# The first 17 microseconds of a fused layernorm, state-space and MLP kernel: reciprocal root on GpSimd, tile 0 scaled by ScalarE, and first matmuls on one x tile

## The chip, the cores and the metric

The kernel runs on one core of a Trainium2 chip. The metric is the device time of one execution in microseconds (us). Besides its time, each timed execution has a span, from its first to its last instruction, which is 1.2 to 1.5 us shorter than the time.

PE is the matrix engine (TensorE), PEld its weight loads, DVE is VectorE, ACT is ScalarE, POOL is GpSimd.

## The reference

The input x is 2048 tokens of 1024 values. It is normalised, and the result goes through a diagonal state-space layer (a recurrence over the tokens) and through a two-layer MLP. Their sum, with x, is the output.

```python
def _layernorm(x, axis=-1, eps=1e-5):
    m = jnp.mean(x, axis=axis, keepdims=True)
    v = jnp.var(x, axis=axis, keepdims=True)
    return (x - m) / jnp.sqrt(v + eps)

# ... _A_ref: complex diagonal recurrence, 1024 states
# ... _B_ref: h = x @ w1 + b1 (3584 wide); act = h * tanh(softplus(h)); act @ w2
    xn = _layernorm(x, axis=-1)
    return x + _A_ref(xn, ...) + _B_ref(xn, ...)
```

## The kernel before

The tokens are worked on in four blocks of 512, each of four x tiles of 128 tokens. Nearly all of the time is a stream of matmuls. Before the stream can start, PE needs normalised and transposed x and the first weights. This stage, the head, is what the change rewrites.

In the head, each x tile passes these steps: its load; `bn_stats` of both halves and `bn_aggr` on VectorE (mean and variance); a root of the variance and a reciprocal; the scaling `(x - m) * y`; eight 128x128 transposes on PE into PSUM; and a copy to SBUF (`xnT`). The weights come in 512 KB ring tiles. Ring tiles 0 and 1 hold the upper and lower half of the contraction (k from 0 to 3, and from 4 to 7) for the weight tiles f = 0 to 3; ring tiles 2 and 3 do so for f = 4 to 7.

Filler matmuls (`keep_busy`) on zeros keep PE occupied while it waits; they are meant to have its clock full when the stream starts.

```python
    def first_sqrt(q):
        aop(lambda e: e.activation(rc(q, 1), mv[:, q, 1:2], AF.Sqrt, bias=kon[:, 2:3]), ...)      # ScalarE

    def first_apply(q, pieces=1):
        y = rc(q, 1)
        vop(lambda e: e.reciprocal(y, y), ...)                                                    # VectorE
        for h in range(pieces):
            ...
            vop(lambda e, d=d: e.tensor_scalar(xn[:, q, d], xx[:, 0, q, d], mv[:, q, 0:1], y,
                                               op0=ALU.subtract, op1=ALU.mult), ...)              # VectorE
    ...
    keep_busy(40)
    for q in range(2):
        first_sums_v(q, 0); first_sums_v(q, 1); first_var_v(q); first_sqrt(q)
    keep_busy(20, [b_mv[0]])          # waits for tile 0's variance
    # transpose of the small parameters on PE
    keep_busy(10, [b_mv[1]])
    first_apply(0)
    first_transpose(0)
    first_apply(1, 2)
    first_transpose(1)
    keep_busy(8)
    # copies of tiles 0 and 1; then statistics, root, scaling of tiles 2 and 3, in this order:
    #   sums 2, var 2, root 2, half of sums 3, scale 2, other half of sums 3, var 3, root 3, scale 3
    for f in range(4):
        first_half(f, 0, 0, NK // 2)                  # tokens of tiles 0 and 1: 256 columns, k 0..3
    for f in range(4):
        first_half(f, 0, NK // 2, NK)                 # k 4..7
        if f == 2:
            first_transpose(2); first_copy(2, AC)
    first_half(4, 0); first_transpose(3); first_copy(3, VE); first_half(5, 0)
    # then the other 256 columns of f = 0..5, and from f = 6 on matmuls of 512 columns
```

"Tokens are columns" here: a matmul of 256 columns covers two x tiles. The layernorm of later blocks (`ln_rsqrt`, a reciprocal root made of 15 VectorE instructions, and `ln_root`, ScalarE's root for block 1) is far from the head.

## Time and profile before

| | before |
|---|---|
| first 3 executions | 621.52 us median (621.43 to 622.23) |
| 6 executions (3 more with the changed kernel) | 621.86 us median (621.43 to 623.07) |
| profiled execution | 621.25 us, span 619.8 us |
| first useful matmul in that profile | 8.55 us |
| stream reaches the second 256 columns of f = 0 | 14.79 us |

The last row is the record of the ninth matmul there, at 14.897 us, less the 0.109 us of a missing record. In this profile every fiftieth matmul or so has no record, and this leaves gaps of exactly two spacings.

These are the span, the busy times and the chain that ended last, from the page of the kernel before.

```profile
span 619.8 us, 7370 instructions
...
PE 613.6 (99%) x2925; PEld 288.3 (47%) x2981; DVE 463.1 (75%) x678; ACT 246.6 (40%) x158; POOL 50.4 (8%) x47
...
PE 95%; ACT 2%; DVE 2%; issue 1%; DVEq 0%
```

PE is busy 99% of the span and holds 95% of the chain. Nothing but PE counts, as long as PE is fed.

This is PE's timeline of the head in the same profile (start us, duration us, engine, line, operation, output and input, count).

```profile
5.02 1.28 PE L463 MATMUL ps<-filler 128*128 128x128 bf16 x20
...
7.02 1.24 PE L379 MATMUL ps<-ident,xn 128*128 128x128 bf16 x16
...
8.55 3.22 PE L509 MATMUL ps<-xnT,ring 128*128 128x256 bf16 x28
11.60 0.61 PE L379 MATMUL ps<-ident,xn 128*128 128x128 bf16 x8
...
13.41 0.61 PE L379 MATMUL ps<-ident,xn 128*128 128x128 bf16 x8
13.86 3.82 PE L509 MATMUL ps<-xnT,ring 128*128 128x256 bf16 x32
```

L463 is the fillers, L379 transposes, L509 the first useful matmuls. From 8.55 us on the entries touch each other: single matmuls start 0.109 us apart (256 columns), transposes 0.056 us apart. So only what lies before 8.55 us can be saved.

This is VectorE's timeline and then ScalarE's one line for the same tile 3, kernel before.

```profile
4.55 0.21 DVE L355 BATCH_NORM_AGGREGATE mv<-stats 128x2 f32<-128x12 f32 x1
...
6.14 0.21 DVE L355 BATCH_NORM_AGGREGATE mv<-stats 128x2 f32<-128x12 f32 x1
...
6.42 0.55 DVE L367 TENSOR_SCALAR xn<-xx,mv,rs 128x1024 bf16<-128x1024 bf16 x1
...
7.98 0.42 DVE L392 COPY xnT<-ps 128x512 bf16<-128x512 bf16 x1 [0.17 <-PE ps L379]
...
11.93 0.21 DVE L355 BATCH_NORM_AGGREGATE mv<-stats 128x2 f32<-128x12 f32 x1
12.50 0.16 DVE L363 RECIPROCAL rs<-rs 128x1 f32<-128x1 f32 x1 [0.36 <-ACT rs L358]
12.70 0.55 DVE L367 TENSOR_SCALAR xn<-xx,mv,rs 128x1024 bf16<-128x1024 bf16 x1
```

```profile
12.17 0.30 ACT L358 ACTIVATE rs<-mv,kon 128x1 f32<-128x1 f32 x1 [1.76 <-DVE mv L355]
```

L355 is the end of a tile's statistics. For tile 3 they end at 11.93 + 0.21 = 12.14 us, ScalarE's root and VectorE's reciprocal follow, and scaling (L367) starts at 12.70: 0.56 us. For tile 0 the scaling waits in VectorE's queue for tile 1's statistics and starts at 6.42 although tile 0's variance was done at 4.76.

### The profile page before, as it was taken

What the parts mean: (1) busy time and instruction counts of PE and PEld (TensorE: products, weight loads), DVE (VectorE), ACT (ScalarE), POOL (GpSimd) and SP (SyncE); (2) the same over time, 40 slices, a digit from 0 to 9 for tenths busy, and PEclk for the clock granted to TensorE, in tenths of its full rate; (3) what the DMA queues carried; (4) which work ended last, traced back from release to release, by engine and by line L of the source; (5) the groups of instructions that cost most, each with busy time, mean ns of one, the idle gap of its engine ahead of it and who ended that gap; (6) DMA issues with size and microseconds to landing.
All of it is one profiled execution on the core that took longest, in us unless ns stands there. A gap on an engine that the chain in (4) does not pass through costs nothing.

```text
span 619.8 us, 7370 instructions
## 1 busy us (share of the span) xinstructions
PE 613.6 (99%) x2925; PEld 288.3 (47%) x2981; DVE 463.1 (75%) x678; ACT 246.6 (40%) x158; POOL 50.4 (8%) x47
## 2 busy tenths in 40 slices
PE   9999999999999999999999999999999999999998
PEld 8544444444444444444444444444444444444444
DVE  6897999999467599998147659999624856999603
ACT  4779996440079940000009992000001999000000
POOL 1999000000100000000010000000000000000000
DMA  8999986840464401783064430276203541033001
GB/s 289 243 214 296 208 160 190 219 136 1 134 194 147 136 1 35 195 209 105 17 186 137 146 126 1 82 205 176 82 34 106 167 169 69 0 122 116 1 0 69
DMA packets 95948, 79.41 MB, mean 128 GB/s; under 512 B 48938, under 2 KB 78506, under 8 KB 95914
## 3 DMA queue, kind: packets, MB, share of 16 engines
q1 hardware_dynamic: 92416, 71.64, 42.3%
q0 software_dynamic: 960, 3.15, 2.2%
q10 hardware_dynamic: 2538, 4.14, 1.8%
q8 instruction: 24, 0.39, 0.3%
q14 instruction: 10, 0.08, 0.0%
HBM read 63.19 MB, written 4.19 MB: 109 GB/s over the span
## 4 chain that ended last, share of the span: by engine, by line
PE 95%; ACT 2%; DVE 2%; issue 1%; DVEq 0%
PE ps L733 49%; PE ps L654 26%; PE ps L675 18%; PE ps L463 1%; PE ps L509 1%; ACT act L635 1%; ACT act L634 1%; ACT act L633 1%; DVE hb L662 0%; DVE stats L350 0%; DVE act L640 0%; PE ps L747 0%; ACT L634 0%; ACT L525 0%; ACT xnT L390 0%
## 5 line engine op out<-in xcount | busy, mean ns | idle before, releaser
L733 PE MATMUL ps<-ring,act 128*128 128x512 bf16 x880 | 193.2, 379 | 0.8
L654 PE MATMUL ps<-xnT,ring 128*128 128x512 bf16 x832 | 182.7, 379 | 0.8
L633 ACT ACTIVATE act<-hb 128x3584 bf16<-128x3584 bf16 x16 | 50.9, 3183 | 224.0 <-DVE hb L662 223.7
L733 PEld LDWEIGHTS ps<-ring,act 128*128 128x128 bf16 x896 | 87.7, 98 | 105.7
L654 PEld LDWEIGHTS ps<-xnT,ring 128*128 128x128 bf16 x848 | 83.0, 98 | 99.9
L662 DVE TENSOR_SCALAR hb<-ps,par 128x512 bf16<-128x512 f32 x112 | 82.2, 747 | 54.6 <-PE ps L654 53.4
L675 PE MATMUL ps<-xnT,BT 128*128 128x512 bf16 x500 | 110.5, 379 | 0.6
L733 PE MATMUL ps<-CT,hT 128*128 128x512 bf16 x494 | 109.2, 379 | 0.6
L680 DVE TENSOR_TENSOR mt<-ps,tab 128x1024 bf16<-128x1024 f32 x64 | 75.4, 1220 | 17.2 <-PE ps L675 16.5
L675 PEld LDWEIGHTS ps<-xnT,BT 128*128 128x128 bf16 x512 | 50.1, 98 | 60.4
L733 PEld LDWEIGHTS ps<-CT,hT 128*128 128x128 bf16 x506 | 49.5, 98 | 59.7
L698 DVE TENSOR_TENSOR_SCAN hT<-cs,qi,hT 128x512 bf16<-128x512 f32 x48 | 58.9, 1269 | 0.0
L778 DVE TENSOR_TENSOR xx<-ps,xx 128x1024 bf16<-128x1024 f32 (+1 forms) x16 | 18.8, 1190 | 46.3 <-PE ps L733 46.2
L634 ACT ACTIVATE act<-act 128x3584 bf16<-128x3584 bf16 x16 | 51.0, 3190 | 0.2
L635 ACT ACTIVATE act<-act 128x3584 bf16<-128x3584 bf16 x16 | 51.0, 3190 | 0.2
L703 DVE TENSOR_TENSOR mt<-hT,tab 128x1024 bf16<-128x1024 bf16 x64 | 41.4, 688 | 1.1
L640 DVE TENSOR_TENSOR act<-act,hb 128x3584 bf16<-128x3584 bf16 x16 | 32.3, 2018 | 1.3 <-ACT act L635 1.3
L287 POOL DMA_DIRECT2D xx<-in_A_x_dram x12 | 6.7, 560 | 254.4 <-DVE xx L778 247.9
L609 ACT ACTIVATE ct<-CT,cs 128x512 f32<-128x512 bf16 x16 | 11.5, 721 | 26.0 <-DVE CT L611 25.9
L634 ACT ACT_TABLE_LOAD x16 | 20.5, 1283 | 0.3
L635 ACT ACT_TABLE_LOAD x16 | 20.5, 1283 | 0.3
L698 DVE TENSOR_TENSOR_SCAN hT<-cs,hT 128x512 bf16<-128x512 f32 x16 | 18.7, 1208 | 0.0
(81 smaller groups left out, 279.2 us busy)
## 6 DMA issues: line engine op xcount, KB each, us to landing
ring<-in_B_w_dram SPq DMA_DIRECT2D x112, 512.0 KB, 4.2
out_dram<-xx ACTq DMA_DIRECT2D x15, 256.0 KB, 2.1
xx<-in_A_x_dram POOLq DMA_DIRECT2D x12, 256.0 KB, 4.6
xx<-in_A_x_dram SPq DMA_DIRECT2D x4, 128.0 KB, 2.2
xx<-in_A_x_dram SPq DMA_DIRECT2D x2, 256.0 KB, 5.2
dsk<-in_A_Dskip_dram SPq DMA_DIRECT2D x1, 256.0 KB, 9.3
xnT<-xn SPq DMA_TRANSPOSE x12, 4.7
BT<-in_A_B_re_dram SPq DMA_TRANSPOSE x8, 6.3
```

Source lines behind the costliest of these rows:

```text
L633: aop(lambda e: e.activation(a, hs, AF.Exp), reads=[b_hb[g % 2]], writes=[b_act[g]])
L634: aop(lambda e: e.activation(a, a, AF.Ln, bias=1.0), reads=[b_act[g]], writes=[b_act[g]])
L635: aop(lambda e: e.activation(a, a, AF.Tanh), reads=[b_act[g]], writes=[b_act[g]])
L640: vop(lambda e: e.tensor_tensor(a, a, hs, op=ALU.mult), reads=[b_act[g], b_hb[g % 2]], writes=[b_act[g]])
L654: PE.mm(lambda e, k=k, w=w: e.matmul(ps[:, bank, :], lhsT=w, rhs=xnT[:, k, :], start=k == 0, stop=k == NK - 1), reads=[b_ring[s]] + b_xnT, ...
L662: vop(lambda e: e.tensor_scalar(hb[:, hs, :], ps[:, bank, :], b1(f), None, op0=ALU.add), reads=[b_ps[bank], b_par], writes=[b_hbf[hs]])
L675: PE.mm(lambda e, j=j, ci=ci, k=k, bank=bank: e.matmul(ps[:, bank + ci, :], lhsT=BT[:, ci, j, k, :], rhs=xnT[:, k, :], start=k == 0, stop= ...
L680: vop(lambda e, s=s, u=u, j=j: e.tensor_tensor(mt[:, s, :, :], u, tab[:, s, j, :].unsqueeze(1).to_broadcast([P, 2, TB]), op=ALU.mult), rea ...
L698: vop(lambda e, ci=ci, init=init: e.tensor_tensor_scan(out=hT[:, ci, j, :], data0=cj("r", j).to_broadcast([P, TB]), data1=hT[:, ci, j, :], ...
L703: vop(lambda e, s=s: e.tensor_tensor(mt[:, s, :, :], hT[:, :, j, :], tab[:, s, j, :].unsqueeze(1).to_broadcast([P, 2, TB]), op=ALU.mult), ...
L733: PE.mm(lambda e: e.matmul(ps[:, u, :], lhsT=lhsT, rhs=rhs, start=st_, stop=last), reads=reads, writes=[b_ps[u]], first=st_, last=last)
L778: vop(lambda e: e.tensor_tensor(xr, src, xr, op=ALU.add), reads=b_ps[bank:bank + n] + [b_x], writes=[b_x])
```

## The change

It means to start the stream earlier, with tile 0 alone. GpSimd computes the reciprocal root as a power of -0.5, so VectorE and ScalarE's tables are not needed for it. ScalarE scales tile 0 while VectorE is still at tile 1's statistics. The first weight tiles run on tile 0's 128 tokens while tile 1 is finished. Since tile 0 and tile 1 now accumulate at different times in one PSUM bank, four matmuls of zeros open the banks. x tile 1 is loaded in one piece instead of two, the loads of x tiles 2 and 3 come after the second ring tile, f = 6 joins the split (`NSPLIT`), fillers are fewer, and the later layernorms use GpSimd's power as well. The core of the diff:

```diff
-    for q in range(2):
-        for h in range(2):
-            SP.dma(... x tile q, half h ...)
+    for h in range(2):
+        SP.dma(... x tile 0, half h ...)
+    load_x(SP, 0, 1)
...
-        if i < 2:
-            load_x(SP, 0, 2 + i)
+        if i == 1:
+            load_x(SP, 0, 2)
+            load_x(SP, 0, 3)
...
-    def first_sqrt(q): ...                     # ScalarE root; reciprocal was in first_apply
+    def first_rstd(q, negated_mean=False):
+        pop(lambda e: e.tensor_scalar(rc(q, 0), mv[:, q, 1:2], EPS, None, op0=ALU.add), ...)
+        pop(lambda e: e.tensor_tensor(rc(q, 1), rc(q, 0), kon[:, 2:3], op=ALU.pow), ...)
+        if negated_mean:
+            pop(lambda e: e.tensor_scalar(rc(q, 2), mv[:, q, 0:1], rc(q, 1), -1.0, op0=ALU.mult, op1=ALU.mult), ...)
...
+                aop(lambda e, d=d: e.activation(xn[:, q, d], xx[:, 0, q, d], AF.Identity, scale=y, bias=nm), ...)
...
-    keep_busy(20, [b_mv[0]])
-    ... parameters' transpose, keep_busy(10, [b_mv[1]])
-    first_apply(0); first_transpose(0); first_apply(1, 2); first_transpose(1); keep_busy(8)
+    keep_busy(14, [b_mv[0]])
+    first_apply(0, 2, AC)
+    first_transpose(0, 0, 4); keep_busy(4); first_transpose(0, 4, NK)
+    ... parameters' transpose
+    for f in range(4):
+        PE.mm(... matmul(ps[:, f, 0:2 * P], lhsT=filler[:, 0:P], rhs=filler[:], start=True, stop=False) ...)
+    ... copies of tile 0, first_apply(1, 2)
+    for f in range(4):
+        first_part(f, 0, 1, 0, NK // 2)               # tile 0 alone, 128 columns
+        if f in (1, 2):
+            first_transpose(1, 4 * (f - 1), 4 * f)
...
+    for f in range(4):
+        first_part(f, 1, 2, 0, NK // 2)               # tile 1 alone
+    for f in range(4):
+        first_part(f, 0, 2, NK // 2, NK)
+    first_part(4, 0, 2, 0, NK // 2); first_transpose(2); first_copy(2, AC)
+    first_part(4, 0, 2, NK // 2, NK); first_part(5, 0, 2)
+    first_transpose(3); first_copy(3, VE); first_part(6, 0, 2)
...
-    def ln_rsqrt(): ...  15 VectorE instructions
-    def ln_root(): ...   ScalarE root, VectorE reciprocal
+    def ln_rstd():
+        pop(... add EPS ...); pop(... op=ALU.pow ...)
```

More of the change, by code (lines that the diff above doesn't have):

```diff
@@ L288, in load_x @@
                   s_xx[i][q] if blk else s_x0[q], writes=[b_xx[i][q]])
-    for q in range(2):
-        for h in range(2):
-            SP.dma(lambda e, q=q, h=h: e.dma_start(xx[:, 0, q, h * 512:(h + 1) * 512],
-                                                   A_x[0, q * P:(q + 1) * P, h * 512:(h + 1) * 512]),
-                   DmaSem(nc, "d_x0%d_%d" % (q, h)), writes=[b_xx[0][q].parts[h]])
+    for h in range(2):
+        SP.dma(lambda e, h=h: e.dma_start(xx[:, 0, 0, h * 512:(h + 1) * 512], A_x[0, 0:P, h * 512:(h + 1) * 512]),
+               DmaSem(nc, "d_x00_%d" % h), writes=[b_xx[0][0].parts[h]])
+    load_x(SP, 0, 1)
     for src, r0, n in ((A_log_dt, 2 * NJ, NJ), (A_Lambda_im, NJ, NJ), (A_Lambda_re, 0, NJ),
@@ L324, in build_kernel @@
         ring_load()
-        if i < 2:
-            load_x(SP, 0, 2 + i)
+        if i == 1:
+            load_x(SP, 0, 2)
+            load_x(SP, 0, 3)
         if i == 5:
             SP.dma(lambda e: e.dma_start(dsk[:], A_Dskip.partition_broadcast(P)), s_dsk, writes=[b_dsk])
-    filler = sb("filler", [P, P], bf16)
+    filler = sb("filler", [P, 2 * P], bf16)
     b_filler = Buf("filler")
@@ L336, in build_kernel @@
                                   compare_op=ALU.is_equal, fill=0.0), reads=[b_ident], writes=[b_ident])
-    for n, v in enumerate((HALF_PI, 0.0, EPS)):
+    for n, v in enumerate((HALF_PI, 0.0, -0.5)):
         pop(lambda e, n=n, v=v: e.memset(kon[:, n:n + 1], v), reads=[b_kon], writes=[b_kon])
@@ L355, in first_var_v, with first_apply @@
         vop(lambda e: e.bn_aggr(mv[:, q, :], stats[:, s, :, :]), reads=[b_stats[s]], writes=[b_mv[q]])
-    def first_sqrt(q):
-        aop(lambda e: e.activation(rc(q, 1), mv[:, q, 1:2], AF.Sqrt, bias=kon[:, 2:3]),
-            reads=[b_mv[q], b_kon], writes=[b_rs1[q]])
-    def first_apply(q, pieces=1):
-        y = rc(q, 1)
-        vop(lambda e: e.reciprocal(y, y), reads=[b_rs1[q]], writes=[b_rs1[q]])
+    def first_rstd(q, negated_mean=False):
+        pop(lambda e: e.tensor_scalar(rc(q, 0), mv[:, q, 1:2], EPS, None, op0=ALU.add),
+            reads=[b_mv[q]], writes=[b_rs1[q]])
+        pop(lambda e: e.tensor_tensor(rc(q, 1), rc(q, 0), kon[:, 2:3], op=ALU.pow),
+            reads=[b_rs1[q], b_kon], writes=[b_rs1[q]])
+        if negated_mean:
+            pop(lambda e: e.tensor_scalar(rc(q, 2), mv[:, q, 0:1], rc(q, 1), -1.0, op0=ALU.mult, op1=ALU.mult),
+                reads=[b_mv[q], b_rs1[q]], writes=[b_rs[q]])
+    def first_apply(q, pieces=1, queue=VE):
+        y, m, nm = rc(q, 1), mv[:, q, 0:1], rc(q, 2)
         for h in range(pieces):
@@ L366, in first_apply @@
             b_x, b_o = (b_xx[0][q], b_xn[q]) if pieces == 1 else (b_xx[0][q].parts[h], b_xn[q].parts[h])
-            vop(lambda e, d=d: e.tensor_scalar(xn[:, q, d], xx[:, 0, q, d], mv[:, q, 0:1], y,
-                                               op0=ALU.subtract, op1=ALU.mult),
-                reads=[b_x, b_mv[q], b_rs1[q]], writes=[b_o])
+            if queue is VE:
+                vop(lambda e, d=d: e.tensor_scalar(xn[:, q, d], xx[:, 0, q, d], m, y, op0=ALU.subtract, op1=ALU.mult),
+                    reads=[b_x, b_mv[q], b_rs1[q]], writes=[b_o])
+            else:
+                aop(lambda e, d=d: e.activation(xn[:, q, d], xx[:, 0, q, d], AF.Identity, scale=y, bias=nm),
+                    reads=[b_x, b_rs[q], b_rs1[q]], writes=[b_o])
     def bank_T(q, k):
@@ L374, in bank_T, with first_transpose @@
         return 6 + q % 2
-    def first_transpose(q):
-        for k in range(NK):
+    def first_transpose(q, k0=0, k1=NK):
+        for k in range(k0, k1):
             bank = bank_T(q, k)
@@ L381, in first_transpose @@
                   reads=[b_xn[q].parts[k // (NK // 2)], b_ident], writes=[b_ps[bank]],
-                  first=k == 0 or bank != bank_T(q, k - 1), last=k == NK - 1 or bank != bank_T(q, k + 1))
+                  first=k == k0 or bank != bank_T(q, k - 1), last=k == k1 - 1 or bank != bank_T(q, k + 1))
     def first_copy(q, queue, k0=0, k1=NK):
@@ L392, in first_copy @@
             vop(lambda e: e.tensor_copy(dst, srcp), reads=[b_ps[bank]], writes=[b_dst])
-    rv = [sb("rv%d" % i, [P, NQ], f32 if i < 3 else i32) for i in range(4)]
-    b_rv = [Buf("rv%d" % i) for i in range(4)]
+    rstd = sb("rstd", [P, NQ], f32)
+    b_rstd = Buf("rstd")
     def ln_stats_only(blk, q):
@@ L403, in ln_stats_only @@
         vop(lambda e: e.bn_aggr(mv[:, q, :], stats[:, s, :, :]), reads=[b_stats[s]], writes=[b_mv[q]])
-    def ln_rsqrt():
-        v, y, t = (rv[n][:, :] for n in range(3))
-        yi, vi, b_i = rv[1][:, :].bitcast(i32), rv[0][:, :].bitcast(i32), rv[3][:, :]
-        vop(lambda e: e.tensor_scalar(v, mv[:, :, 1], EPS, None, op0=ALU.add), reads=b_mv, writes=[b_rv[0]])
-        vop(lambda e: e.tensor_scalar(b_i, vi, 1, None, op0=ALU.logical_shift_right),
-            reads=[b_rv[0]], writes=[b_rv[3]])
-        vop(lambda e: e.tensor_scalar(yi, b_i, -1.0, float(0x5f3759df), op0=ALU.mult, op1=ALU.add),
-            reads=[b_rv[3]], writes=[b_rv[1]])
-        for _ in range(3):
-            vop(lambda e: e.tensor_tensor(t, y, y, op=ALU.mult), reads=[b_rv[1]], writes=[b_rv[2]])
-            vop(lambda e: e.tensor_tensor(t, t, v, op=ALU.mult), reads=[b_rv[0], b_rv[2]], writes=[b_rv[2]])
-            vop(lambda e: e.tensor_scalar(t, t, -0.5, 1.5, op0=ALU.mult, op1=ALU.add),
-                reads=[b_rv[2]], writes=[b_rv[2]])
-            vop(lambda e: e.tensor_tensor(y, y, t, op=ALU.mult), reads=[b_rv[1], b_rv[2]], writes=[b_rv[1]])
-    def ln_root():
-        y = rv[1][:, :]
-        aop(lambda e: e.activation(y, mv[:, :, 1], AF.Sqrt, bias=kon[:, 2:3]), reads=b_mv + [b_kon], writes=[b_rv[1]])
-        vop(lambda e: e.reciprocal(y, y), reads=[b_rv[1]], writes=[b_rv[1]])
+    def ln_rstd():
+        pop(lambda e: e.tensor_scalar(rstd[:, :], mv[:, :, 1], EPS, None, op0=ALU.add), reads=b_mv, writes=[b_rstd])
+        pop(lambda e: e.tensor_tensor(rstd[:, :], rstd[:, :], kon[:, 2:3].to_broadcast([P, NQ]), op=ALU.pow),
+            reads=[b_rstd, b_kon], writes=[b_rstd])
     def ln_scale(blk, q):
         i = blk % 2
-        vop(lambda e: e.tensor_scalar(xn[:, q, :], xx[:, i, q, :], mv[:, q, 0:1], rv[1][:, q:q + 1],
+        vop(lambda e: e.tensor_scalar(xn[:, q, :], xx[:, i, q, :], mv[:, q, 0:1], rstd[:, q:q + 1],
                                       op0=ALU.subtract, op1=ALU.mult),
-            reads=[b_xx[i][q], b_mv[q], b_rv[1]], writes=[b_xn[q]])
+            reads=[b_xx[i][q], b_mv[q], b_rstd], writes=[b_xn[q]])
     def ln_skip(blk, q):
@@ L462, in keep_busy @@
         for i in range(n):
-            PE.mm(lambda e: e.matmul(ps[:, 3, 0:P], lhsT=filler[:], rhs=filler[:], start=True, stop=True),
+            PE.mm(lambda e: e.matmul(ps[:, 3, 0:P], lhsT=filler[:, 0:P], rhs=filler[:, 0:P], start=True, stop=True),
                   reads=[b_filler] + (list(behind) if i == 0 else []), writes=[b_ps[3]], first=i == 0, last=i == n - 1)
-    keep_busy(40)
-    aop(lambda e: e.activation(rs[:, :, 3], kon[:, 2:3].to_broadcast([P, NQ]), AF.Sqrt), reads=[b_kon], writes=b_rs)
+    keep_busy(36)
+    aop(lambda e: e.activation(rs[:, :, 3], kon[:, 1:2].to_broadcast([P, NQ]), AF.Exp), reads=[b_kon], writes=b_rs)
     for q in range(2):
@@ L471, in build_kernel, with w1_tile, first_part @@
         first_var_v(q)
-        first_sqrt(q)
-    keep_busy(20, [b_mv[0]])
-    PE.op(lambda e: e.transpose(ps16(2)[:, 0:NST], st[:, :], ident[0:NST, 0:NST]),
-          reads=[b_st, b_ident], writes=[b_ps[2]])
-    keep_busy(10, [b_mv[1]])
-    first_apply(0)
-    first_transpose(0)
-    first_apply(1, 2)
-    first_transpose(1)
-    keep_busy(8)
-    first_copy(0, AC, 0, 4)
+        first_rstd(q, q == 0)
+    keep_busy(14, [b_mv[0]])
+    first_apply(0, 2, AC)
+    first_transpose(0, 0, 4)
+    keep_busy(4)
+    first_transpose(0, 4, NK)
+    PE.op(lambda e: e.transpose(ps16(5)[:, 0:NST], st[:, :], ident[0:NST, 0:NST]),
+          reads=[b_st, b_ident], writes=[b_ps[5]])
+    for f in range(4):
+        PE.mm(lambda e, f=f: e.matmul(ps[:, f, 0:2 * P], lhsT=filler[:, 0:P], rhs=filler[:], start=True, stop=False),
+              reads=[b_filler], writes=[b_ps[f]], first=True, last=False)
+    first_copy(0, VE, 0, 4)
+    aop(lambda e: e.copy(par[:, :], ps16(5)[:, 0:NST]), reads=[b_ps[5]], writes=[b_par])
+    first_copy(0, AC, 4, NK)
+    first_apply(1, 2)
+    NSPLIT = 7
+    def w1_tile(base, f, k):
+        s = (base + 2 * (f // 4) + k // (NK // 2)) % NRING
+        wt = ring[:, s, :].rearrange("p (k f) -> p k f", k=NK // 2)
+        return s, wt[:, k % (NK // 2), (f % 4) * P:(f % 4 + 1) * P]
+    def first_part(f, q0, q1, k0=0, k1=NK):
+        ts = slice(q0 * P, q1 * P)
+        for k in range(k0, k1):
+            s, w = w1_tile(0, f, k)
+            PE.mm(lambda e, k=k, w=w: e.matmul(ps[:, f, ts], lhsT=w, rhs=xnT[:, k, ts],
+                                               start=k == 0 and (f >= 4 or q0 == 2), stop=k == NK - 1),
+                  reads=[b_ring[s]] + [b.parts[k // 4] for b in b_xnT[q0:q1]], writes=[b_ps[f]],
+                  first=f >= 4 and q0 == 0 and k == 0, last=q1 == NQ and k == NK - 1)
+    for f in range(4):
+        first_part(f, 0, 1, 0, NK // 2)
+        if f in (1, 2):
+            first_transpose(1, 4 * (f - 1), 4 * f)
     first_copy(1, VE, 0, 4)
-    first_copy(0, AC, 4, NK)
     first_copy(1, AC, 4, NK)
-    vop(lambda e: e.tensor_copy(par[:, :], ps16(2)[:, 0:NST]), reads=[b_ps[2]], writes=[b_par])
     for h in range(2):
@@ L489, in build_kernel @@
     first_var_v(2)
-    first_sqrt(2)
+    first_rstd(2)
     first_sums_v(3, 0)
@@ L494, in build_kernel @@
     first_var_v(3)
-    first_sqrt(3)
+    first_rstd(3)
     first_apply(3)
-    NSPLIT = 6
-    def w1_tile(base, f, k):
-        s = (base + 2 * (f // 4) + k // (NK // 2)) % NRING
-        wt = ring[:, s, :].rearrange("p (k f) -> p k f", k=NK // 2)
-        return s, wt[:, k % (NK // 2), (f % 4) * P:(f % 4 + 1) * P]
-    def first_half(f, half, k0=0, k1=NK):
-        ts = slice(half * 256, half * 256 + 256)
-        for k in range(k0, k1):
-            s, w = w1_tile(0, f, k)
-            PE.mm(lambda e, k=k, w=w: e.matmul(ps[:, f, ts], lhsT=w, rhs=xnT[:, k, ts],
-                                               start=k == 0, stop=k == NK - 1),
-                  reads=[b_ring[s]] + [b.parts[k // 4] for b in b_xnT[2 * half:2 * half + 2]], writes=[b_ps[f]],
-                  first=half == 0 and k == 0, last=half == 1 and k == NK - 1)
     for f in range(4):
-        first_half(f, 0, 0, NK // 2)
+        first_part(f, 1, 2, 0, NK // 2)
     for f in range(4):
-        first_half(f, 0, NK // 2, NK)
-        if f == 2:
-            first_transpose(2)
-            first_copy(2, AC)
-    first_half(4, 0)
+        first_part(f, 0, 2, NK // 2, NK)
+    first_part(4, 0, 2, 0, NK // 2)
+    first_transpose(2)
+    first_copy(2, AC)
+    first_part(4, 0, 2, NK // 2, NK)
+    first_part(5, 0, 2)
     first_transpose(3)
     first_copy(3, VE)
-    first_half(5, 0)
+    first_part(6, 0, 2)
     aop(lambda e: e.activation(c("dt"), ldt, AF.Exp), reads=[b_par], writes=[b_cs["dt"]])
@@ L650, in first_tile @@
         if blk == 0 and f < NSPLIT:
-            first_half(f, 1)
+            first_part(f, 2, NQ)
         for k in range(0 if blk == 0 and f < NSPLIT else NK):
@@ L838, in build_kernel @@
                 ln_stats_only(blk + 1, q)
-            ln_rsqrt()
+            ln_rstd()
             for q in range(NQ):
@@ L845, in build_kernel @@
                 mish_mul(3)
-                ln_root()
+                ln_rstd()
                 for q in range(NQ):
```

## The prediction

> **What bounds the kernel now.** TensorE: the page gives PE 99% busy and 95% of the chain that ended last. In the timeline the first useful matmul (L509, 256 columns) starts at 8.55 us; from there to 617.7 us they follow every 0.109 us (256 columns) or 0.216 us (512), with no stall over 0.1 us except missing records. So time is saved only before 8.55 us, or lost by a new PE stall. The layernorm of later blocks, the square-root table load and VectorE's 15-operation reciprocal root lie under a full PE: worth 0.
>
> **The head before.** Tile 0's variance is done at 4.76 us, but its scaling (0.55 us) waits in VectorE's queue behind tile 1's statistics (to 6.35) and a reciprocal, and ends at 6.96. Transposes 7.02 to 8.1, copies to 8.5. The first matmuls need both tiles. First halves of 6 weight tiles and all four x tiles' transposes are done at 14.79.
>
> **The head after, costed.**
> - GpSimd chain, from 4.76: hand-over 0.09, add 0.2, power 0.35, scale of the mean 0.2, gaps 0.06. Estimates: a 128x1 GpSimd MEMSET took 0.10 us, a dependent one started 0.06 later, 128x512 operations took 1.27 to 1.94. The power was never run here; it is the largest unknown. Ready near 5.75.
> - ScalarE scales 512 columns: estimate 0.80 us from the Trainium skill, "ScalarE: Activation LUTs", section "What ACT_TABLE_LOAD costs" (186 ns + 0.833 ns per element + 93 ns per pointer operand, here two). The trace agrees on other cases: 0.59 us for a 512-column copy, 0.295 for one element with a bias. First half ready at 6.6, second about 7.05.
> - Transposes, the parameters' transpose and four zero matmuls (4 x 0.109): PE is busy to about 7.8; tile 0's first half is copied about 7.5. First useful matmul near 7.8, 0.75 us earlier.
> - But tile 1's transposes (0.45 us), formerly in the waiting time, now stand inside the useful stream, and 16 matmuls of 256 columns become 32 of 128 (0.056 each, as transposes show; +0.04). Net lead about 0.3 us.
> - Two things can take it back. Weight tiles are paced by DMA: they land 1.5 us apart, ring tile 3 at 12.92, where the kernel before already waited; I expect 12.6 to 12.9, needed near 12.7. And tiles 2 and 3 follow tile 1's later copy (9.1 instead of 8.40), with the GpSimd chain about as long as root plus reciprocal (0.56 to 0.66): tile 3 is scaled near 14.1 to 14.4 (before 13.25), wanted near 14.1. Stall 0 to 0.3 us.
>
> **Sum.** The same work is done at about 14.6 to 14.8 against 14.79: gain 0.0 to 0.3 us. Afterwards PE streams as before. I predict 621.3 us, range 620.4 to 622.2; faster by over 2% 0.01, within 2% 0.98, slower 0.01.
>
> **Signs.** First useful matmul at 7.5 to 8.1; power at 0.2 to 0.5 us; PE stalls before the transposes of tiles 2 and 3, or at ring tile 3, of up to 0.5 us; after 16 us no new PE gap; one table load fewer on ScalarE before 16 us.
>
> **What would make it wrong.** A power of over 1 us (every tile's chain passes it): slower by about 1 us. A power near 0.1 us and weight tiles landing 0.4 us earlier: up to 0.6 us faster. A clock that turns full later, as PE now pauses nearly 1 us after its fillers: up to 1 us slower.

## The result

The changed kernel takes 622.55 us (622.40 to 622.60, 6 executions) against 621.86 us. The ratio is 1.0008, with a 95% interval from 0.9996 to 1.0021. The predicted range ended at 622.2 us. A gain of 0.0 to 0.3 us was forecast; the medians lie 0.7 us and the means 0.6 us on the other side, and the interval just includes no loss.

The same lines of the page after:

```profile
span 621.3 us, 7413 instructions
...
PE 616.8 (99%) x2985; PEld 289.0 (47%) x2985; DVE 457.7 (74%) x642; ACT 242.5 (39%) x152; POOL 57.6 (9%) x62
...
PE 97%; DVE 1%; POOL 0%; DMA 0%; ACT 0%; issue 0%; DVEq 0%; ACTq 0%; POOLq 0%
```

PE's larger busy time is mostly that of the records which the profile before lacks, not of more work.

PE's timeline of the head after. L386 is transposes, L474 the zero matmuls, L493 the useful ones (the counts merge 128 and 256 columns). The brackets give PE's idle time and what ended it.

```profile
7.20 0.40 PE L386 MATMUL ps<-ident,xn 128*128 128x128 bf16 x4 [0.52 <-ACT xn L375]
...
8.37 0.61 PE L474 MATMUL ps<-filler 128*128 128x256 bf16 x4
8.81 0.61 PE L493 MATMUL ps<-xnT,ring 128*128 128x128 bf16 x8
...
13.35 0.62 PE L386 MATMUL ps<-ident,xn 128*128 128x128 bf16 x8
...
15.81 0.62 PE L386 MATMUL ps<-ident,xn 128*128 128x128 bf16 x8 [0.53 <-DVE xn L372]
16.27 1.45 PE L493 MATMUL ps<-xnT,ring 128*128 128x256 bf16 x11
```

The useful stream starts at 8.81 us, later than the 8.55 us before. It then stops twice. Single records give a wait of 0.10 us in front of tile 2's transposes (13.35) and 0.69 us in front of tile 3's (15.81); the bracket counts less, because a matmul's modelled end runs into the wait. Work that before was done at 14.79 us is done at 16.27 us, 1.48 us later, and the profiled spans differ by 1.5 us. Nothing else moved: from 25 to 615 us PE has no gap in either profile except missing records.

The 1.48 us are this sum: +0.27 (start), +0.45 (tile 1's eight transposes now inside the stream), +0.04 (narrow matmuls), +0.79 (the two waits), -0.10 (waits that the kernel before had); 0.03 are left over.

The chain that ended last, in order of time (start us, duration us, what), shows what the second wait is made of. "issue" is time without a visible wait.

```profile
13.93 0.22 DVE mv L355
...
14.23 0.23 POOL rs L358
...
14.54 0.58 POOL rs L360
...
15.21 0.56 DVE xn L372
...
15.81 0.62 PE ps L386 x8
```

From the end of tile 3's statistics (13.93 + 0.21 = 14.14) to the start of its scaling (15.21) there are now 1.07 us, where root and reciprocal took 0.56. The same for tile 2: 1.07 against 0.66. And the start of this stretch is itself late, because VectorE gets to tile 2's statistics only after tile 1's copy, which ends at 10.11 us instead of 8.40. (Tile 2's load is not what it waits for: it had landed at 9.28.) Tile 3's scaling starts 2.51 us later than before (15.21 against 12.70): 1.59 from the later start of tile 2's statistics, 0.41 from tile 2's longer chain, behind which the second half of tile 3's statistics stands in VectorE's queue, and 0.51 from tile 3's own. PE would have taken tile 3 at 15.12 us. An estimate from these figures: without the 0.92 us of the two chains the scaling ends at 14.84, in time.

GpSimd's timeline for tile 0, and ScalarE's, show the late start.

```profile
4.97 0.24 POOL L358 TENSOR_SCALAR rs<-mv 128x1 f32<-128x1 f32 x1 [2.06 <-DVE mv L355]
5.29 0.58 POOL L360 TENSOR_TENSOR rs<-rs,kon 128x1 f32<-128x1 f32 x1
5.97 0.27 POOL L363 TENSOR_SCALAR rs<-mv,rs 128x1 f32<-128x1 f32 x1
```

```profile
6.34 1.52 ACT L375 ACTIVATE xn<-xx,rs 128x512 bf16<-128x512 bf16 x2 [2.40 <-POOL rs L363]
```

The power took 0.58 us, the whole GpSimd chain 4.88 to 6.24. ScalarE's two pieces took 0.81 and 0.80 us, started 0.72 apart, and the second ended at 7.85. VectorE, to which the work was not given, has nothing to do from 6.41 to 7.64 us.

### The profile page after: what moved, and what is told of

Its sections match the earlier page's. It is cut to its first block, busy times and chain, and to the rows that moved or that the text cites. A ratio compares the mean times of both kernels' runs of the same rounds, so it can differ in the third digit from the quotient of the medians.

```text
span 621.3 us, 7413 instructions
## 1 busy us (share of the span) xinstructions
PE 616.8 (99%) x2985; PEld 289.0 (47%) x2985; DVE 457.7 (74%) x642; ACT 242.5 (39%) x152; POOL 57.6 (9%) x62
## 4 chain that ended last, share of the span: by engine, by line
PE 97%; DVE 1%; POOL 0%; DMA 0%; ACT 0%; issue 0%; DVEq 0%; ACTq 0%; POOLq 0%
PE ps L735 49%; PE ps L656 29%; PE ps L677 18%; PE ps L493 1%; DVE stats L350 1%; DMA xx<-in_A_x_dram 0%; POOL rs L360 0%; ACT xn L375 0%; PE ps L749 0%; PE ps L386 0%; DVE xn L372 0%; POOL rs L358 0%; DVE mv L355 0%; PE ps L474 0%; DVE xx L803 0%
```

## The experiments

All ten runs gave correct results. Five executions each were timed, in rounds with nine of the kernel before on the same chip.

| run | what | us, median (range) | before | ratio (95%) | spans |
|---|---|---|---|---|---|
| a_again | the change, again | 622.55 (622.48 to 622.87) | 622.04 | 1.0009 (0.9997 to 1.0022) | 621.2 to 621.6 |
| b_again | before, again | 622.30 (621.74 to 622.37) | 621.93 | 1.0004 (0.9991 to 1.0018) | 620.3 to 621.0 |
| a_root23 | change, roots for tiles 2, 3 | 621.61 (621.59 to 621.82) | 621.93 | 0.9996 (0.9984 to 1.0009) | 620.4 to 620.6 |
| a_zeros | change, zeros earlier | 622.09 (621.97 to 622.99) | 621.93 | 1.0006 (0.9993 to 1.0018) | 620.7 to 621.7 |
| b_pow | before, with the power | 622.49 (622.33 to 622.97) | 621.93 | 1.0011 (0.9999 to 1.0024) | 621.1 to 621.7 |
| a_dve0 | change, VectorE scales tile 0 | 622.18 (621.83 to 622.51) | 622.04 | 1.0003 (0.9990 to 1.0015) | 620.6 to 621.3 |
| b_fill | before, fewer fillers | 621.70 (621.34 to 621.84) | 622.04 | 0.9994 (0.9980 to 1.0007) | 619.9 to 620.4 |
| a_best | three repairs | 621.36 (621.00 to 621.57) | 622.04 | 0.9988 (0.9976 to 1.0001) | 619.8 to 620.3 |
| a_best_order | the same, old load order | 621.20 (621.08 to 621.47) | 621.77 | 0.9990 (0.9976 to 1.0004) | 619.8 to 620.2 |
| a_mid | change, VectorE's root in the middle | 622.47 (622.44 to 622.50) | 621.77 | 1.0010 (0.9997 to 1.0022) | 621.2 to 621.3 |

All differences are below 0.2%, and no interval excludes 1. The verdicts therefore rest on positions in the traces, which move as a cause says or don't, and on whole sets of spans. The kernel before, 27 times, had spans of 620.1 to 621.3 us.

### Controls

> Control: the changed kernel, unchanged, on the chip of the following runs. Expected: times within 0.3 us of 622.5, span 621.2 to 621.4, wait of 0.69 us before tile 3's transposes again.

> Control: the kernel before, unchanged, as a second profile. Its six times scattered from 621.4 to 623.1 us where the changed kernel's stayed within 0.2 us. Expected: profiled span 619.8 to 621, ratio 1.000. If the scatter is in the head, first useful matmul or the first use of a weight tile will stand elsewhere than at 8.55 and 12.96 us.

The changed kernel repeats: spans 621.2 to 621.6 (621.2 to 621.4 expected), and again 0.69 us before tile 3's transposes. The kernel before does not. Its second profile, PE's timeline of the head:

```profile
4.11 3.37 PE L463 MATMUL ps<-filler 128*128 128x128 bf16 x31
7.42 0.20 PE L474 MATMUL ps<-ident,st 52*128 52x52 bf16 x1
...
8.19 1.06 PE L379 MATMUL ps<-ident,xn 128*128 128x128 bf16 x16
...
9.63 3.22 PE L509 MATMUL ps<-xnT,ring 128*128 128x256 bf16 x28
```

The first useful matmul comes at 9.63 us, 1.08 later than in the first profile, although tile 0 was scaled at the same 6.42 us. The single fillers tell why. In the first profile their spacing falls from 0.107 to 0.056 us at 4.00 us. In this one it falls at 6.87 us. So the first forty fillers end later, the twenty behind tile 0's variance start at 5.64 us instead of 5.02 and run at half clock until 6.87, and the transposes wait behind all of them. The Trainium skill, "TensorE: Matmul & The Clock Gate", section "What's actually happening", says that the clock is released by a free-running window of activity, so that the moment varies. No run here shows the window itself; the moment does vary, by more than the page's ±0.5 us. In the changed kernel this costs nothing: in four profiles that keep its beginning (the first, a_again, a_root23 and a_mid) the spacing falls at 6.30, 3.86, 4.18 and 5.3 us, and the useful stream starts at 8.81, 8.74, 8.87 and 8.73. The consequence is that the profile on which the prediction was built, span 619.8, was shorter than all 27 later spans of the same kernel. The difference of the two first profiles, 1.5 us, overstates the loss; the medians' 0.5 to 0.7 us is the typical one.

### The power, alone and undone

Two theories of the wait before tile 3's transposes are tested: G says that GpSimd's chain is too long, S that everything merely starts too late.

> The kernel before, with only one part of the change: GpSimd's add and power in place of root and reciprocal for the four tiles of the head. Theory G: tile 1 scaled 0.35 us later, so first useful matmul at 8.9; wait before tile 3's transposes about 0.6 us; span 0.9 us above that of before, some 620.7. Theory S: span within 0.3 us of before.

> The changed kernel, with tiles 2 and 3 back on ScalarE's square root and VectorE's reciprocal. Theory G (GpSimd's latency on the path of each tile): the PE wait before tile 3's transposes, 0.69 us, falls to under 0.1, the one before tile 2's, 0.10, goes, and the span falls from 621.3 to about 620.5. Theory S (tile 3 is late because tile 1's copy now comes 1.7 us later): the wait before tile 3's transposes falls by less than half, span about 621.0.

The edit of b_pow puts GpSimd's add and power in `first_sqrt` of the kernel before, and drops the reciprocal:

```diff
     def first_sqrt(q):
-        aop(lambda e: e.activation(rc(q, 1), mv[:, q, 1:2], AF.Sqrt, bias=kon[:, 2:3]), ...)
+        pop(lambda e: e.tensor_scalar(rc(q, 0), mv[:, q, 1:2], EPS, None, op0=ALU.add), ...)
+        pop(lambda e: e.tensor_tensor(rc(q, 1), rc(q, 0), kon[:, 3:4], op=ALU.pow), ...)
```

The edit of a_root23, on the changed kernel:

```diff
-    first_rstd(2)
+    first_root(2)            # ScalarE: Sqrt(var + EPS)
     first_sums_v(3, 0)
+    first_inverse(2)         # VectorE: reciprocal
...
-    first_rstd(3)
+    first_root(3)
+    first_inverse(3)
```

PE's timeline of b_pow, and then of a_root23:

```profile
9.08 3.22 PE L510 MATMUL ps<-xnT,ring 128*128 128x256 bf16 x28
...
14.75 0.62 PE L380 MATMUL ps<-ident,xn 128*128 128x128 bf16 x8 [0.53 <-DVE xn L368]
```

```profile
8.87 0.61 PE L500 MATMUL ps<-xnT,ring 128*128 128x128 bf16 x8
...
13.31 0.61 PE L393 MATMUL ps<-ident,xn 128*128 128x128 bf16 x8
...
15.06 0.61 PE L393 MATMUL ps<-ident,xn 128*128 128x128 bf16 x8
```

In the old structure the power alone makes the wait before tile 3's transposes, 0.69 us by the single records. It also makes a wait of 0.16 us before tile 2's and, as tile 1's scaling starts 0.53 us later, a first useful matmul at 9.08 us (8.9 expected; 8.55 in the first profile). So the span, 621.2 us (some 620.7 expected, 0.9 above the first profile's 619.8), doesn't measure the wait at tile 3 by itself. It is 0.7 above the 620.5 that is the median of before on that chip, and the five spans (621.1 to 621.7) lie above all fourteen of the kernel before (620.2 to 621.0). In the new structure, taking the power away from tiles 2 and 3 removes both waits; tile 3's scaling ends at 14.89 us. The start, 8.87 us, has not moved, and the span falls by 0.7 us, to 620.6 (620.5 expected). All five spans (620.4 to 620.6) are below those of the changed kernel. Theory G holds for tiles 2 and 3; the expectation of theory S, a wait that shrinks by less than half, fails.

### The zero matmuls and ScalarE's scaling

> The changed kernel, with the four zero matmuls issued before tile 0's transposes, in PE's wait, instead of after them. Theory S (start of the useful stream sets everything after it): first useful matmul at 8.37 instead of 8.81 us, and the whole of the head follows, tile 3's wait unchanged at 0.7; span about 620.9. Theory G or a DMA bound: the start moves but the wait before tile 3's transposes grows by as much, span 621.3.

> The changed kernel, with tile 0 scaled by VectorE after tile 1's statistics, as the kernel before did, and without GpSimd's scale of the mean. Theory V (giving tile 0 to ScalarE gained nothing, as VectorE stands idle from 6.4 to 7.6 us anyway): halves ready at 6.85 and 7.2 instead of 7.15 and 7.85, first useful matmul at 8.05 instead of 8.81, span about 0.7 us shorter, 620.6. Rival (ScalarE's offload is worth what it was meant for): first useful matmul later than 8.8 and span longer.

In a_zeros the four zero matmuls move up in PE's queue, and the four fillers between tile 0's transposes go to another bank:

```diff
     keep_busy(14, [b_mv[0]])
+    for f in range(4):
+        PE.mm(... zeros into bank f ...)
     first_apply(0, 2, AC)
...
-    keep_busy(4)
+    keep_busy(4, bank=7)
...
-    for f in range(4):
-        PE.mm(... zeros into bank f ...)
```

In a_dve0 VectorE scales tile 0, as before:

```diff
-        first_rstd(q, q == 0)
+        first_rstd(q)
...
-    first_apply(0, 2, AC)
+    first_apply(0, 2)
```

PE's timeline of a_zeros, and then of a_dve0:

```profile
8.29 0.62 PE L493 MATMUL ps<-xnT,ring 128*128 128x128 bf16 x8
...
12.69 0.61 PE L493 MATMUL ps<-xnT,ring 128*128 128x256 bf16 x4 [0.22 <-DMA ring<-in_B_w_dram]
13.75 0.62 PE L386 MATMUL ps<-ident,xn 128*128 128x128 bf16 x8 [0.45 <-DVE xn L372]
...
16.20 0.62 PE L386 MATMUL ps<-ident,xn 128*128 128x128 bf16 x8 [0.53 <-DVE xn L372]
```

```profile
8.24 0.61 PE L493 MATMUL ps<-xnT,ring 128*128 128x128 bf16 x8
...
12.97 0.62 PE L386 MATMUL ps<-ident,xn 128*128 128x128 bf16 x8
...
15.43 0.62 PE L386 MATMUL ps<-ident,xn 128*128 128x128 bf16 x8 [0.53 <-DVE xn L372]
```

The zeros cost what they last: the stream starts at 8.29 us instead of 8.81 (0.08 of this is an earlier landing of x), and four of the five spans are 620.7 to 620.9 (620.9 expected, 621.3 without the edit). The fifth, 621.7, is the profiled one. There the loads from ring tile 1 to ring tile 3 landed about 1.1 us later than in the first profile of the change: ring tile 2 at 12.64 us instead of 11.47, for which PE waited 0.39 us, and x tile 2 at 10.38 instead of 9.28, so that VectorE's statistics of tile 2 began at 10.41 and PE waited another 0.62 us in front of tile 2's transposes. This profile can't show the gain; the other four spans do. The wait before tile 3's transposes is again 0.69 us, as expected under theory S: a later start and the longer chain both cost time, at different places. So an earlier start is passed on, but only as far as the loads allow.

In a_dve0, VectorE has tile 0's halves ready at 6.83 and 7.15 us, ScalarE had them at 7.15 and 7.85. The stream starts at 8.24 us (8.05 expected; x tile 1 landed 0.17 us later than in the first profile of the change, and the scaling stands behind its statistics). The profiled span is 620.9 (620.6 expected), and 620.9 is the median of the five spans too, where a_again, on the same chip, has 621.3. Of the 0.57 us at the start 0.4 are left; the wait before tile 2's transposes grew from 0.10 to 0.29 us, as tile 2's load again came last. The rival is out: ScalarE's part made the head longer.

### The repairs together, and the load order

> All three repairs: tiles 2 and 3 on root and reciprocal, zero matmuls in PE's wait, tile 0 scaled by VectorE; fewer fillers in front of it. If the causes add: first useful matmul at 7.75 us, no wait over 0.1 us before the transposes, but a wait of up to 0.4 us for ring tile 3 or tile 2's load, which now come last; span about 619.8, 0.7 us below the typical kernel before. If DMA already bounds the head: waits of 0.7 us or more at the weight tile or at tile 2, span 620.3.

> The repaired kernel, with the load order of the kernel before (x tile 2 after the first ring tile, x tile 3 after the second). Theory D (the repaired head is bounded by the bytes that have to land before ring tile 3): the 0.33 us wait before tile 2's transposes goes, as its load lands near 8.3 us, but the wait for ring tile 3 (landing 13.25) grows by as much; span unchanged at 620.0 to 620.2. Rival (order matters): span 0.3 us shorter.

The version a_best joins the edits of a_root23, a_zeros and a_dve0, cuts `keep_busy(14)` to 8 and drops `keep_busy(4)`. (As in a_root23, the table that ScalarE loads at the start is that of the root again.) In a_best_order the loads of x tiles 2 and 3 stand after the first and second ring tile, as in the kernel before. PE's timelines, a_best first:

```profile
7.74 0.61 PE L499 MATMUL ps<-xnT,ring 128*128 128x128 bf16 x8 [0.26 <-DVE xnT L406]
...
12.51 0.62 PE L393 MATMUL ps<-ident,xn 128*128 128x128 bf16 x8
13.30 1.49 PE L499 MATMUL ps<-xnT,ring 128*128 128x256 bf16 x12 [0.17 <-DMA ring<-in_B_w_dram]
14.62 0.61 PE L393 MATMUL ps<-ident,xn 128*128 128x128 bf16 x8
```

```profile
7.55 0.61 PE L498 MATMUL ps<-xnT,ring 128*128 128x128 bf16 x8 [0.16 <-DVE xnT L405]
...
11.98 0.61 PE L392 MATMUL ps<-ident,xn 128*128 128x128 bf16 x8
13.02 1.48 PE L498 MATMUL ps<-xnT,ring 128*128 128x256 bf16 x12 [0.42 <-DMA ring<-in_B_w_dram]
```

The causes nearly add: the start is at 7.74 us (7.75 expected), tile 3's wait is gone, and the spans are 619.8 to 620.3 us (619.8 expected) where the kernel before had 620.3 to 620.9 on the same chip. By the single records PE waits 0.27 us before tile 2's transposes and 0.33 us for ring tile 3, whose last piece landed at 13.25. With the old load order the first wait disappears and the wait for ring tile 3, landing at 12.97, grows to 0.58 us. The span is 0.3 us shorter in the profile, but its start was also 0.2 earlier (the clock turned full at 5.3 us instead of 6.5), and the sets, from two chips, (619.8 to 620.3, and 619.8 to 620.2) are the same. In both profiles the last thing that the head waits for is the landing of ring tile 3, and the load order only chooses where the rest of the wait is seen. These two versions are the only ones with a median clearly under that of the kernel before, by 0.6 to 0.7 us (a_root23 and b_fill have 0.3); the intervals just reach 1, so the gain is likely and not proved.

### The fillers, and the later layernorms

> The kernel before, with 20, 10 and 8 filler matmuls cut to 12, 4 and 4. Theory F (its scatter of about 1 us comes from fillers that run at half clock in some executions and stand in front of the transposes; the second profile showed 9.63 instead of 8.55 us for the first useful matmul): all spans at or below 620.0 and within 0.3 us of each other. Rival (the scatter is DMA's): spread and median unchanged, 620.2 to 620.9.

> The changed kernel, with VectorE's 14-operation root put back for the layernorm of blocks 1 to 3 (in block 1 too). The prediction said that this part of the change is worth 0, as PE streams without a gap there. Expected: VectorE busy some 6 us longer, no PE gap after 25 us, span 621.2 to 621.4. Rival: if VectorE bounds the stretch between projection and recurrence, span over 622.

```diff
-    keep_busy(20, [b_mv[0]])
+    keep_busy(12, [b_mv[0]])
...
-    keep_busy(10, [b_mv[1]])
+    keep_busy(4, [b_mv[1]])
...
-    keep_busy(8)
+    keep_busy(4)
```

With fewer fillers (b_fill) the kernel before starts its stream at 8.58 us although the clock turned full only at 4.75 us. Its spans, 619.9 to 620.4, lie 0.3 us under those of before. But they still scatter by 0.5 us, and only one of the five is at or below the 620.0 that theory F had for all of them. The profile shows waits of 0.24 us for tile 2 and 0.30 us for ring tile 3 (landing 13.45). So theory F is shown for the one slow start of b_again and likely for part of the scatter; the landing times may be the rest. How much each has in an execution without a profile stays open.

The run a_mid puts `ln_rsqrt` back, for block 1 too. (It has 15 instructions; the 14 of the expectation is a slip.) VectorE's busy time on the page:

```profile
PE 613.4 (99%) x2929; PEld 288.6 (46%) x2985; DVE 465.1 (75%) x687; ACT 242.6 (39%) x152; POOL 53.6 (9%) x56
```

VectorE is busy 7.4 us longer than after the change (465.1 against 457.7), and the spans are 621.2 to 621.3. The later layernorms are worth nothing, as predicted.

## Why the prediction was wrong

- **Right: what bounds the kernel.** PE streams from the head to the end, the middle of the change is worth 0 (a_mid), and all of the result lies before 17 us.
- **Wrong: the size of the GpSimd chain.** The step "power 0.35 us" measured 0.57 to 0.58, outside the 0.2 to 0.5 given as a sign. The sum for tile 0 was to end at 5.75 us and ended at 6.24, of which 0.12 is x's later landing. For tiles 2 and 3 the step "the GpSimd chain about as long as root plus reciprocal" is the one that failed: 1.07 us each against 0.66 and 0.56. An add of 0.22, a power of 0.57 and three hand-overs of 0.08 to 0.11 make it, where ScalarE's root of 0.30 and VectorE's reciprocal of 0.16 were handed over in 0.03 to 0.04 each. The 0.69 us wait before tile 3's transposes (the signs allowed up to 0.5) follows from this. It disappears without the power (a_root23) and appears with the power alone (b_pow).
- **Wrong: ScalarE's second half.** One piece was predicted at 0.80 us and took 0.81. But the second was to be ready 0.45 us after the first, and came 0.71 after. The cited section of "ScalarE: Activation LUTs" also states that back-to-back instructions overlap by about 93 ns, which would have given 0.71; the prediction didn't use it.
- **Wrong as a sum: the first useful matmul.** Predicted for 7.8 us, measured 8.81. About 0.1 us is x's later landing, 0.4 the GpSimd chain, 0.3 ScalarE's two pieces, and 0.2 the transposes and zero matmuls behind them, which took 0.96 us from the scaled second half to the first useful matmul instead of 0.75.
- **Right in kind: the lead is eaten later.** Tile 1's transposes inside the stream cost 0.45 us as costed. Ring tile 3 landed at 12.96 us (12.6 to 12.9 predicted) but PE reached it late and never waited for it. Tile 1's copy ended at 10.11 instead of the predicted 9.1; with this and the longer chains of tiles 2 and 3, tile 3 was scaled at 15.76 us instead of 14.1 to 14.4.
- **Not seen: the profile before was a fast execution.** The full clock came 2.87 us earlier in it than in the control. The changed kernel, with fewer fillers in front of its transposes, lost nothing when its clock turned full at 6.30 us (with 3.86, in a_again, it started only 0.07 us earlier); the prediction had listed a late clock as a danger.

The typical loss of 0.5 to 0.7 us is thus the power's 0.7 us at tiles 2 and 3: without it, the spans are those of the kernel before again. At the start, ScalarE's scaling and the place of the zero matmuls use up what the earlier start on tile 0 would have given.

## What to carry to other kernels

Moving a tiny operation to an idle engine pays only if its whole chain, with the hand-overs in and out, is shorter on the path that waits for it; time one such operation on that engine before building a pipeline on it. Check first whether the engine that is to be relieved isn't idle at that very moment, and put work that needs no data, like opening banks, into a wait instead of behind it. When the expected gain is below 1 us, take two or three profiles of the kernel before: here its start differed by 1.08 us between two of them.

## What the Trainium skill lacked or had wrong

- "GPSIMD Engine Reference", section "Elementwise — side-by-side cycle accounting", has times for 512 and 2048 elements and no total for GpSimd's dispatch; no page has the power. Measured at 128x1: add 0.22 to 0.27 us (once 0.40, in b_pow), power 0.57 to 0.60, two-step multiply 0.27, and 0.08 to 0.11 us between dependent instructions, on GpSimd as well as from it and to it. Between VectorE and ScalarE, in the kernel before, it was 0.03 to 0.04 us.
- "TensorE: Matmul & The Clock Gate", section "What you observe", puts the change to the full clock about 4 us into the activity, ±0.5 us from run to run. With fillers from 1.04 or 1.11 us on, it came 2.75 us (a_again), 2.96 (first profile), 3.7 (b_fill), 5.2 (after) and 5.83 us (b_again) later. In the last two the fillers had paused for 0.35 us before, so their activity was not quite sustained. The page doesn't warn that warm-up matmuls that run at half clock delay the work queued behind them; here by 1.08 us.
- "ScalarE: Activation LUTs", section "What ACT_TABLE_LOAD costs", was right in both figures: 0.81 and 0.80 us for 512 columns with two pointer operands (0.80 by its formula), and an overlap of 0.093 us.
